# Attention and two expert layers on one core: another issue order for the five engines up to the last chunk

## The chip, the core and the metric

The kernel runs on one core of a Trainium2 chip. The metric is the device time of one execution in microseconds (us). The core's engines have a queue each and run side by side: TensorE (PE, matrix products; PEld is its loading of weights), VectorE (DVE), ScalarE (ACT), GpSimd (POOL), and SyncE (SP), which issues transfers (DMA). An engine takes its instructions in the order of its queue; one that must wait for another engine's result holds up all that stand behind it.

## The reference

Causal attention with a decay (4 batches, 8 heads, 576 positions, head size 64), whose output is the input of a feed-forward layer with a hard swish, whose output goes to a layer of eight experts, of which each token takes the one with the highest logit:

```python
scores = scale * np.matmul(q, k.transpose(0, 1, 3, 2))
decay = cum[:, :, :, None] - cum[:, :, None, :]
scores = np.where(causal, -1000000000.0, scores + decay)
attn = np.exp(scores - np.max(scores, axis=-1, keepdims=True))
attn = attn / (np.sum(attn, axis=-1, keepdims=True) + 1e-09)
x = np.matmul(attn, v)            # then 2304 tokens of 512
...
h = x @ w_in                      # 512 x 2048
g = h * np.clip(h + 3.0, 0.0, 6.0) / 6.0
x = g @ w_out                     # 2048 x 512
...
e_idx = np.argmax(x @ w_gate, axis=1)
h = np.maximum(x[mask] @ w1[e], 0.0)       # 512 x 1024
out[mask] = gate_w[mask, None] * eom[mask, e, None] * (h @ w2[e])
```

## The kernel before, in words

**Three parts.** The tokens are cut into six chunks of 384. Part one is the attention, in units of two heads and 128 positions. Part two is the feed-forward layer (`moe1_steps`), chunk by chunk; a chunk can start when all attention outputs of its tokens are there, so attention of later chunks and feed-forward products of earlier ones share the engines. Part three is the experts. To be precise enough, each factor is kept as a high part in f16 and a low part in bf16 or f16, and each product is made of three.

**An attention unit.** PE makes the scores (L457, L524, L525) in one of three PSUM tiles `sc`. DVE adds the mask and takes the row's extreme (L504, or L530 for the last positions; tile `nm`), and so frees the score tile. ACT takes the exponential (L538) and writes its high part (L555, L559, L560), POOL or DVE the low part (L556, L563). SP transposes both by DMA (L567, `pt` from `pn`). PE multiplies with the values (L590 to L592, and L602 to L605 for the last positions): these are the probability products, "pv" below, with 65 columns each. They have a single accumulator in PSUM, `ps_pv`. DVE empties it: L613 and L614 take the reciprocal of the row's sum, L615 multiplies (`evac`); for the last positions it is L627, L628 and two instructions of L631, one for each half (`evac_last`). ACT (L618) and POOL split the result `xs` into `xn`, and SP transposes that into the chunk's `xT` (L653). L399 on ACT copies rows of the keys and queries, L376 splits loaded ones.

**A feed-forward chunk.** For each of 16 steps twelve products of 384 columns (L857) fill one of three PSUM banks `mm`. ACT adds 3 and cuts at zero (L861), DVE multiplies with the bank (L864) and so gives the bank back, ACT writes the high part of `g` (L865), DVE or POOL the low part (L869). Then 4 times 48 products (L880), emptied by L889 (ACT) and L890 (DVE). The first weights come as f32 and are converted in the kernel: `conv_raw` gathers bits on DVE (L820, L822, L824), ACT writes the high part (L827), POOL or DVE the low part (L828). The gates of a chunk (`gate_steps`) are small products (L945, L977, L978) and much bookkeeping on DVE (L959 to L1000, among it the cast L994), with PSUM tiles from the same three banks `mm`.

**What sets the order.** The program is traced once, and each engine's instructions are numbered in traced order. `ORDER` (L58 to L195) holds for each of the five engines a list of runs over those numbers: "a+n" is a and the next n. `pin_order` ties each instruction to the one ahead of it in this list, so the engine issues in that order. It is called behind the tracing of the last chunk's feed-forward layer and covers all ahead of that call: 4274 of PE's products. The experts (`first = [expert1...]` and on) stand behind it, in an order of their own. `pin_order` changes no dependence between engines: an instruction that needs another engine's result waits for it wherever it stands.

Of the kernel before, what the change touches and what calls it, by code (L numbers as in the profile page):

```python
# [60 lines left out]
        "0+43 48+7 59+3 44+3 66+3 56+2 63+2 96+1 70+6 98+4 77+7 103+1 112+8 85+3 93+2 89+3 105+3 121+3 137+3 "  # L61
        "109+2 125 128+8 144+8 126+1 141+2 157 160+8 176+1 158+1 178+6 153+3 169+3 185+3 201+3 173+2 189+2 "
        "205+2 221+2 217+3 233+3 249+3 192+8 208+8 265+3 368+1 237+2 382+1 253+2 269+2 224+8 240+8 308+2 "
        "256+8 272+35 311+8 420+8 320+25 429 346+1 430+1 440+11 348+19 370+7 396+9 378+3 384+11 406+10 418+1 "
        "417 432+7 452+11 480+9 464+1 490+1 526+10 492+1 537 466+6 506+7 473+6 554+11 538+1 580+11 566+1 "
        "592+3 494+11 514+11 540+13 596+3 612+11 688+3 676+11 704+7 724+3 692+11 568+11 600+11 624+13 752 "
        "712+11 777 802 753+2 778+2 803+2 728+23 765+5 638+37 815+3 771+5 790+5 828+6 840 796 835+4 866+5 "
        "797+1 872 841 853+1 842 855 843 856 873+4 756+5 799 891+8 800+1 900+1 878+3 902 916+23 762 940+2 "
        "903+3 943+2 1024+2 763+1 781+8 1027 946+24 806+8 819+8 971+21 1049+3 993 1074+1 844+8 857+8 1076+1 "
        "994+18 1099+3 1013+1 1160+1 882+8 907+8 1015+8 1183+1 1206+3 1028+8 1053+8 1078+8 1103+8 1210+3 "  # L70
        "1037+11 1062+6 1235+1 1069+4 1087+7 1162+8 1185+8 1264+1 1095+3 1112+4 1290+7 1117+11 1322+1 1129+4 "
        "1214+8 1237+8 1134+25 1171+10 1350+1 1388+7 1266+11 1298+11 1324+13 1182 1194 1420+1 1195+10 1223+11 "
        "1460+1 1246+5 1486+7 1352+11 1396+11 1422+13 1252+6 1606 1259+4 1278+11 1310+3 1622 1314 1607+2 "
        "1623+1 1462+11 1494+11 1530+13 1625 1638+3 1315+6 1338+11 1364+11 1762+3 1544+23 1376+10 1568+13 "
        "1387 1408+11 1838+3 1863+3 1888+1 1436+23 1842+5 1890+1 1913 1474+11 1506+23 1582+6 1594 1589+1 "
        "1595+8 1591 1604+1 1610 1592+1 1611+10 1626+11 1642+33 1848 1676 1849 1677 1850 1678+7 1867 1686 "
        "1868 1687 1869 1688 1870 1689 1871 1690 1872 1691 1873 1692 1874 1693 1875 1694+22 1914 1717 1915 "
        "1892+6 1718 1899 1719 1900 1916 1720+6 1917 1727 1918 1728 1919 1729 1920 1730 1921 1731 1922 1732 "
        "1923 1733 1924 1734 1925 1735+17 1944 1753 1945 1754 1946 1755 1947 1756+5 1948+1 1766 1950 1767 "
        "1951 1768 1952 1769 1953 1969 1770 1954 1771 1955 1970 1772 1956 1971 1773 1972 1774+3 1973+2 1778 "  # L80
        "1976 1779 1977 1780 1978 1781 1979 1994 1782 1980 1783 1981 1995 1784 1996 1785 1997 1786+7 2019 "
        "1794 2020 1795 2021 1796 2022 1797+17 1998+8 2023+8 1815+22 2080+3 2105+3 1851+11 2084+7 1876 2092 "
        "1877+6 2109 1884 2110 1885 2111 1886 2112 1887 2130 2113 2131 2114 2132 2115 2133 2116 1901 2117 "
        "1902+6 2155 1909 2156 1910 2157 1911 2158 1912 1926+3 2180 1930 2181 1931 2203+1 1932+4 2134+8 "
        "2159+8 1937+1 2226+7 1939+4 1957+4 2255+1 1962+5 2182+8 2205+8 1968 2278 1982 2279 1983+10 2304+7 "
        "2007+2 2234+8 2257+8 2010+8 2032+11 2432 2448 2433 2044+3 2280+11 2312+11 2048+31 2449 2434+9 "
        "2093+11 2118+11 2143+11 2168+9 2474+7 2444 2178 2445 2179 2446 2191 2447 2192+9 2506 2202 2507 "
        "2214+11 2243+4 2450+11 2482+11 2508+10 2248 2519 2249 2520 2250 2521 2251+3 2266+11 2292+11 2324+20 "
        "2582 2345 2583 2346+5 2584 2352 2585 2353 2586 2354 2587 2355 2588 2356 2589 2357 2590 2358 2591 "
        "2359 2592 2360 2593 2361 2594 2362 2595 2363+8 2608+7 2372+11 2616 2384 2617 2385 2618 2386 2619 "  # L90
        "2387 2620 2388 2621 2389 2622 2390 2623 2391 2624 2392 2625 2393 2626 2394 2627 2395+27 2658 2423 "
        "2659 2424 2660 2425 2661 2426 2662 2427 2663 2428 2664 2429 2665 2430 2666 2431 2667+2 2462 2670 "
        "2463 2671 2464+1 2722 2466 2723 2467 2724 2468 2725 2469+4 2494+3 2738 2498 2739 2499 2740 2500 2741 "
# [1362 lines left out]
```

## Time and profile before

| | us |
|---|---|
| median of three runs | 810.03 |
| lowest and highest | 807.61, 811.63 |
| the profiled execution | 808.86 |
| its span | 807.1 |
| PE busy in the span | 726.0 |
| DVE busy | 471.5 |
| ACT busy | 450.9 |
| POOL busy | 315.6 |

The span is the time from the first to the last record of the execution's trace; 1.8 us of the profiled execution lie around it. Busy time is counted without time in which an engine waits. A group of matmuls of one kind is shown as one row with its count; its length includes the tail of the last one, which overlaps what follows. The number in square brackets behind a row is the idle time of the engine ahead of it, with the instruction that ended it. The granted clock is TensorE's: 1.00 is 2.4 GHz and 0.50 is 1.2 GHz. The first feed-forward product runs at 73.35 us.

### The profile page before, as it was taken

What the parts mean: (1) busy time and instruction counts of PE and PEld (TensorE: products, weight loads), DVE (VectorE), ACT (ScalarE), POOL (GpSimd) and SP (SyncE); (2) the same over time, 40 slices, a digit from 0 to 9 for tenths busy, and PEclk for the clock granted to TensorE, in tenths of its full rate; (3) what the DMA queues carried; (4) which work ended last, traced back from release to release, by engine and by line L of the source; (5) the groups of instructions that cost most, each with busy time, mean ns of one, the idle gap of its engine ahead of it and who ended that gap; (6) DMA issues with size and microseconds to landing.
All of it is one profiled execution on the core that took longest, in us unless ns stands there. A gap on an engine that the chain in (4) does not pass through costs nothing. (4 is left out here: it accounts for less than half of the span.)

```text
span 807.1 us, 16599 instructions
## 1 busy us (share of the span) xinstructions
PE 726.0 (90%) x6166; PEld 474.6 (59%) x6177; DVE 471.5 (58%) x1267; ACT 450.9 (56%) x909; POOL 315.6 (39%) x393
## 2 busy tenths in 40 slices
PE   4755979889899999998999889999999999999995
PEld 2533546556556655665666555666677766756862
DVE  7998987646751585229723968573142575536520
ACT  4864779857893676368824646552123465535430
POOL 9556778766663353245712420000042232220010
PEclk9986989999999999999999999999999999999999
DMA  8758799989986585469724737723068889968210
GB/s 246 221 171 200 173 198 243 211 148 165 176 162 137 121 145 115 67 124 159 131 42 91 139 79 233 245 67 105 1 168 148 237 266 295 302 200 258 82 39 28
DMA packets 263778, 127.95 MB, mean 159 GB/s; under 512 B 214658, under 2 KB 247522, under 8 KB 263684
## 3 DMA queue, kind: packets, MB, share of 16 engines
q1 hardware_dynamic: 251860, 105.20, 58.9%
q0 software_dynamic: 4960, 15.73, 6.1%
q10 hardware_dynamic: 6864, 5.80, 2.6%
q8 instruction: 54, 0.88, 0.5%
q14 instruction: 40, 0.33, 0.1%
HBM read 71.52 MB, written 10.08 MB: 101 GB/s over the span
## 5 line engine op out<-in xcount | busy, mean ns | idle before, releaser
L857 PE MATMUL mm<-xT,wi 128*128 128x384 f16 (+1 forms) x1152 | 209.3, 333 | 10.3 <-DMA xT<-xn 5.4
L880 PE MATMUL mm<-g,wo 128*128 128x384 f16 (+1 forms) x1152 | 195.7, 326 | 1.5 <-DVE hr L864 1.4
L857 PEld LDWEIGHTS <-wi 128*128 128x128 f16 (+1 forms) x1152 | 112.2, 99 | 85.2 <-issue 16.4
L880 PEld LDWEIGHTS <-wo 128*128 128x128 f16 (+1 forms) x1152 | 111.0, 98 | 73.6 <-issue 1.8
L1160 PEld LDWEIGHTS <-W 128*128 128x128 f16 (+1 forms) x1344 | 99.9, 98 | 9.1 <-issue 0.6
L556 POOL TENSOR_TENSOR pn<-ms,pn 128x384 bf16<-128x384 f32 (+1 forms) x80 | 82.6, 1037 | 56.2 <-ACT pn L555 53.2
L538 ACT ACTIVATE ms<-ms,nm 128x512 f32<-128x512 f32 (+4 forms) x144 | 79.3, 576 | 34.2 <-DVE nm L504 26.6
L1160 PE MATMUL mm<-g,W 128*128 128x256 f16 (+3 forms) x1152 | 96.6, 246 | 0.5 <-DVE wo L1164 0.5
L1179 PE MATMUL mm<-W,wo 128*128 128x512 f16 (+1 forms) x422 | 94.2, 379 | 2.4 <-ACTq L1392 1.6
L1051 DVE TENSOR_TENSOR W<-stw,W 128x1024 bf16<-128x1024 f32 x46 | 55.6, 1223 | 52.5 <-ACT W L1050 52.4
L504 DVE CUSTOM_DVE_ANT_1 ms<-sc,mask 128x128 f32<-128x128 f32 (+3 forms) x128 | 59.2, 485 | 26.5 <-PE sc L457 12.7
L1179 PEld LDWEIGHTS <-wo 128*128 128x128 f16 (+1 forms) x432 | 41.9, 98 | 52.1 <-issue 2.0
L869 DVE TENSOR_TENSOR g<-hr,g 128x384 bf16<-128x384 f32 x80 | 54.9, 688 | 29.6 <-ACT g L865 29.4
L864 DVE SCALAR_TENSOR_TENSOR hr<-hr,mm 128x384 f32<-128x384 f32 x96 | 52.7, 549 | 28.7 <-ACT hr L861 28.0
L1186 POOL DMA_INDIRECT out_dram<-wo,ids x18 | 18.0, 998 | 119.8 <-ACT wo L1185 96.5
L865 ACT ACTIVATE g<-hr 128x384 f16<-128x384 f32 x96 | 49.3, 516 | 27.3 <-DVE hr L864 26.6
L861 ACT ACTIVATE hr<-mm,bias 128x384 f32<-128x384 f32 x96 | 54.5, 568 | 16.3 <-PE mm L857 14.6
L1164 DVE SCALAR_TENSOR_TENSOR wo<-mm,wo 128x128 bf16<-128x128 f32 (+1 forms) x96 | 33.3, 356 | 46.9 <-ACT wo L1163 44.4
L590 PE MATMUL pv<-vt,pt 128*128 128x65 f16 x320 | 41.8, 197 | 20.6 <-DVE xs L615 9.8
L1050 ACT ACTIVATE W<-stw 128x1024 f16<-128x1024 f32 x46 | 47.7, 1050 | 14.5 <-DMA stw<-in_moe_w_dram 13.9
L890 DVE SCALAR_TENSOR_TENSOR x<-mm,x 128x384 bf16<-128x384 f32 x24 | 13.2, 555 | 71.9 <-ACT x L889 71.9
L457 PE MATMUL sc<-K,q 128*128 128x256 f16 (+2 forms) x192 | 46.1, 297 | 9.2 <-DVE nm L504 6.5
(191 smaller groups left out, 1179.8 us busy)
## 6 DMA issues: line engine op xcount, KB each, us to landing
stw<-in_moe_w_dram SPq DMA_DIRECT2D x46, 512.0 KB
stx<-in_moe_w_dram SPq DMA_DIRECT2D x18, 512.0 KB
wo<-in_moe_w_in_dram SPq DMA_DIRECT2D x16, 512.0 KB
raw<-in_moe_w_out_dram ACTq DMA_DIRECT2D x11, 512.0 KB
rows<-rw POOLq DMA_DIRECT2D x15, 256.0 KB, 2.9
ldk<-in_k_dram SPq DMA_DIRECT2D x14, 256.0 KB
ldq<-in_q_dram SPq DMA_DIRECT2D x14, 256.0 KB
ldv<-in_v_dram SPq DMA_DIRECT2D x13, 256.0 KB
```

Source lines behind the costliest of these rows:

```text
L504: nc.vector.tensor_tensor_reduce(out=pairs(ms[:, off:off + w]), in0=ps[:, 0:w].rearrange("p (c j) -> p c j", c=2), in1=pairs(mask[:, 640 - ...
L538: nc.scalar.activation(out=ms[:, off:off + w], in_=ms[:, off:off + w], func=AF.Exp, scale=-1.0, bias=nm[:, i:i + 1])
L556: nc.gpsimd.tensor_tensor(out=lo.bitcast(BF16), in0=ms[:, 0:N], in1=hi, op=ALU.subtract)
L857: nc.tensor.matmul(ps[:, 0:w], lhsT=l.bitcast(BF16) if a else l, rhs=r.bitcast(BF16) if b2 else r, start=i == 0, stop=i == 3 * KD - 1)
L861: nc.scalar.activation(out=hr, in_=ps[:, 0:w], func=AF.Relu, bias=bias3)
L864: nc.vector.scalar_tensor_tensor(out=hr, in0=hr, scalar=6.0, in1=ps[:, 0:w], op0=ALU.min, op1=ALU.mult)
L865: nc.scalar.activation(out=g[:, m, 0, 0:w], in_=hr, func=AF.Copy)
L869: either.tensor_tensor(out=g[:, m, 1, 0:w].bitcast(BF16), in0=hr, in1=g[:, m, 0, 0:w], op=ALU.subtract)
L880: nc.tensor.matmul(ps[:, 0:w], lhsT=l.bitcast(BF16) if a else l, rhs=r.bitcast(BF16) if b2 else r, start=i == 0, stop=i == 3 * NF - 1)
L1051: nc.vector.tensor_tensor(out=lo.bitcast(BF16), in0=sts[i], in1=hi, op=ALU.subtract)
L1160: nc.tensor.matmul(ps[:, 0:w], lhsT=l.bitcast(BF16) if a else l, rhs=r.bitcast(BF16) if b2 else r, start=i == 0, stop=i == 3 * KD - 1)
L1179: nc.tensor.matmul(ps, lhsT=l.bitcast(BF16) if a else l, rhs=r.bitcast(BF16) if b2 else r, start=i == 0, stop=i == 3 * NF2 - 1)
```

## The change

Only the strings in `ORDER` differ: the same numbers, every one once, in another succession, on all five engines. The new table is seven lines shorter, so that each line behind it has a number lower by seven (L864 of before is L857 of after). A line of it before and after:

```diff
 ORDER = {
     "PE":
-        "0+43 48+7 59+3 44+3 66+3 56+2 63+2 96+1 70+6 98+4 77+7 103+1 112+8 85+3 93+2 89+3 105+3 121+3 137+3 "
...
+        "0+31 48+7 59+3 32+15 66+3 56+2 96+1 63+2 70+6 98+4 89+3 103+1 112+8 105+3 77+11 121+3 93+2 109+2 "
...
```

PE's first difference is at its 33rd product and its last at the 4254th, near 580 us. Counted as runs of products of one kind, PE's order has 729 before and 490 after; pv products that stand alone between two feed-forward products are 190 before and 37 after. Of the other engines' instructions 829 of 1131 stand elsewhere on DVE, 525 of 766 on ACT, 208 of 359 on POOL and 165 of 326 on SP.

Three places, the first on DVE, about 108 to 112 us of the trace before. `pv_1246` is the accumulator that is emptied, `raw`, `cv`, `w32` and `wo` belong to the conversion of weights; a trailing number tells tiles of one name apart. Before, from L627 on:

```order
L627 TENSOR_SCALAR rl_1364<-pv_1246 128x2
L530 ISA ms_1433,nm_1434<-sc_1441,mask4_85,nm_1434 128x64
L530 ISA nm_1434 128x1
L824 SCALAR_TENSOR_TENSOR w32_1155<-raw_1085,cv_1156 128x512
L628 RECIPROCAL rl_1364<-rl_1364 128x2
L828 TENSOR_TENSOR wo_99<-w32_1116,wo_99 128x4x128
L820 TENSOR_SCALAR cv_1217<-raw_1123 128x512
L631 TENSOR_SCALAR xs_1365<-pv_1246,rl_1364 64x64 x2
```

After, from the same instruction on (L620 is L627 of before, L624 is L631, L813 is L820, L821 is L828):

```order
L620 TENSOR_SCALAR rl_1364<-pv_1246 128x2
L523 ISA ms_1433,nm_1434<-sc_1435,mask_84 128x2x256
L523 ISA nm_1434 128x1
L621 RECIPROCAL rl_1364<-rl_1364 128x2
L813 TENSOR_SCALAR cv_1156<-raw_1085 128x512
L624 TENSOR_SCALAR xs_1365<-pv_1246,rl_1364 64x64
L497 ISA ms_1521,nm_1522<-sc_1523,mask_84 128x2x256
L497 ISA nm_1522 128x1
L523 ISA ms_1433,nm_1434<-sc_1441,mask4_85,nm_1434 128x64
L523 ISA nm_1434 128x1
L624 TENSOR_SCALAR xs_1365<-pv_1246,rl_1364 64x64
```

L828 of `w32_1116` stood between L628 and the two L631, and now stands four rows below the last of these; one L820 is now between L628 and the first L631, and parts of an L504 and an L530 between the two L631.

The second is on ACT, about 308 to 313 us. `hr` is the feed-forward step's tile, `mm` its bank, `K2`, `kp` and `Q2`, `qp` are the next keys and queries. Before:

```order
L861 ACTIVATE hr_4255<-mm_4242,bias3_86 128x384
L399 ACTIVATE K2_94<-K1_93 64x1024
L376 ACTIVATE kp_5251<-ldk_4266 128x8x64
L538 ACTIVATE ms_4860<-ms_4860,nm_4861 128x512
L865 ACTIVATE g_97<-hr_4255 128x384
L399 ACTIVATE Q2_0_88<-q1_5116 64x1024
L376 ACTIVATE qp_5258<-ldq_4274 128x8x64
L861 ACTIVATE hr_4289<-mm_4276,bias3_86 128x384
```

After (L854 is L861 of before, L392 is L399, L369 is L376):

```order
L854 ACTIVATE hr_4255<-mm_4242,bias3_86 128x384
L392 ACTIVATE K2_94<-K1_93 64x1024
L854 ACTIVATE hr_4289<-mm_4276,bias3_86 128x384
L369 ACTIVATE kp_5251<-ldk_4266 128x8x64
L531 ACTIVATE ms_4860<-ms_4860,nm_4861 128x512
L858 ACTIVATE g_97<-hr_4255 128x384
```

L861 of `mm_4276` stood last of these, behind L399 of `Q2_0` and both L376, and now is the third, behind L399 of `K2`; the L399 of `Q2_0` stands 23 rows below it.

The third is on DVE, about 371 to 376 us, where a chunk's gates are worked out among feed-forward steps. Before:

```order
L864 SCALAR_TENSOR_TENSOR hr_5100<-hr_5100,mm_5087 128x384
L988 TENSOR_SCALAR z_5275<-z_5275 128x3
L990 TENSOR_TENSOR z_5275<-z_5275,sx_5276 128x3
L869 TENSOR_TENSOR g_97<-hr_5100,g_97 128x384
L991 RECIPROCAL z_5275<-z_5275 128x3
L994 CAST vb_5287<-z_5275 128x3
L995 CAST vals_108<-vb_5287 128x3
L864 SCALAR_TENSOR_TENSOR hr_5135<-hr_5135,mm_5122 128x384
```

After (L857 is L864 of before, L987 is L994):

```order
L857 SCALAR_TENSOR_TENSOR hr_5135<-hr_5135,mm_5122 128x384
L974 TENSOR_REDUCE z_5275<-t3_5171 128x3
L964 TENSOR_TENSOR ohsum_107<-ohsum_107,oh_106 128x8
L862 TENSOR_TENSOR g_97<-hr_5100,g_97 128x384
L975 TENSOR_REDUCE sx_5276<-t2_5170 128x3
L982 TENSOR_SCALAR sx_5276<-sx_5276 128x3
L981 TENSOR_SCALAR z_5275<-z_5275 128x3
L983 TENSOR_TENSOR z_5275<-z_5275,sx_5276 128x3
L984 RECIPROCAL z_5275<-z_5275 128x3
L987 CAST vb_5287<-z_5275 128x3
L988 CAST vals_108<-vb_5287 128x3
L857 SCALAR_TENSOR_TENSOR hr_5195<-hr_5195,mm_5182 128x384
```

L864 of `mm_5122` stood behind the cast L994 of `z_5275`, and now stands nine rows ahead of it; the next L864, of `mm_5182`, stands two rows behind the cast.

## Rows read from the trace of the kernel before

**Rows 1.** The page's head: engine, busy us (share of the span) x instructions.
```profile
PE 726.0 (90%) x6166; PEld 474.6 (59%) x6177; DVE 471.5 (58%) x1267; ACT 450.9 (56%) x909; POOL 315.6 (39%) x393
```

**Rows 2.** By stage: start:end, length, busy PE, PEld, DVE, ACT, POOL, granted clock.
```profile
0.00:73.35 73.35, 38.33 (x333) 27.29 (x334) 66.22 (x163) 44.61 (x93) 46.15 (x82) 0.86 0.75 213
73.35:480.00 406.65, 372.18 (x3262) 236.77 (x3262) 250.93 (x771) 268.88 (x567) 218.72 (x262) 0.98 0.75 142
480.00:800.00 320.00, 315.54 (x2573) 210.49 (x2581) 154.36 (x335) 137.42 (x250) 49.76 (x49) 1.00 0.59 170
```

**Rows 3.** The same view of seven stretches of the second stage.
```profile
100.00:135.00 35.00, 28.76 (x240) 18.39 (x239) 29.14 (x84) 28.92 (x62) 28.73 (x33) 0.90 1.12 219
140.00:150.00 10.00, 7.55 (x57) 4.63 (x55) 8.51 (x26) 9.23 (x20) 7.82 (x9) 1.00 1.24 254
160.00:180.00 20.00, 15.84 (x172) 10.15 (x171) 9.02 (x35) 12.59 (x30) 13.45 (x21) 0.97 0.74 153
195.00:230.00 35.00, 29.50 (x297) 19.65 (x294) 24.53 (x88) 30.13 (x66) 23.39 (x29) 0.95 0.97 174
285.00:315.00 30.00, 26.98 (x250) 16.68 (x247) 21.34 (x67) 24.21 (x50) 16.36 (x20) 1.00 0.90 157
360.00:405.00 45.00, 39.64 (x376) 26.42 (x372) 35.14 (x114) 38.57 (x90) 28.42 (x36) 0.96 0.80 141
450.00:475.00 25.00, 18.66 (x205) 12.53 (x203) 20.68 (x65) 13.38 (x31) 11.52 (x17) 1.00 0.59 110
```

**Rows 4.** PE's waits, 75 to 480 us: us in total, times, longest.
```profile
PE pv L590 <- DVE xs L631: 7.4, 4, 3.7
...
PE mm L857 <- DVE hr L864: 4.8, 3, 1.8
```

**Rows 5.** Busy time in four stretches at the low clock: the first, the sum.
```profile
110.60:117.40 6.80, 5.25 (x49) 3.98 (x50) 6.75 (x16) 3.76 (x9) 5.69 (x7) 0.50 1.18 175
...
sum 17.00, PE 15.18 PEld 9.74 DVE 12.58 ACT 11.03 POOL 9.32; mean PE 3.79 PEld 2.43 DVE 3.15 ACT 2.76 POOL 2.33
```

**Rows 6.** DVE in order of time, 105 to 112 us: start, length, instruction.
```profile
105.38 0.69 DVE L820 TENSOR_SCALAR cv<-raw 128x512 int32<-128x512 int32 x1 [1.06 <-DMA raw<-in_moe_w_out_dram]
...
107.45 0.15 DVE L627 TENSOR_SCALAR rl<-pv 128x2 f32<-128x2 f32 x1
...
109.25 1.67 DVE L828 TENSOR_TENSOR wo<-w,wo 128x512 bf16<-128x512 f32 x1 [0.77 <-ACT wo L827]
...
111.44 0.57 DVE L631 TENSOR_SCALAR xs<-pv,rl 64x64 f32<-64x64 f32 x2
```

**Rows 7.** PE in order of time, at 112 us.
```profile
112.15 0.21 PE L590 MATMUL pv<-vt,pt 128*128 128x65 f16 x1 [3.67 <-DVE xs L631]
```

**Rows 8.** ACT in order of time, 311 to 313 us.
```profile
311.06 1.05 ACT L399 ACTIVATE Q<-q 64x1024 f16<-64x1024 f16 x1
...
312.66 0.56 ACT L861 ACTIVATE hr<-mm,bias 128x384 f32<-128x384 f32 x1
```

**Rows 9.** DVE in order of time, 299 to 378 us.
```profile
299.97 0.56 DVE L864 SCALAR_TENSOR_TENSOR hr<-hr,mm 128x384 f32<-128x384 f32 x1
...
373.16 2.40 DVE L994 CAST vb<-z 128x3 bf16<-128x3 f32 x1
...
377.40 0.55 DVE L864 SCALAR_TENSOR_TENSOR hr<-hr,mm 128x384 f32<-128x384 f32 x1
```

**Rows 10.** PE in order of time, 296 to 370 us.
```profile
296.16 0.33 PE L857 MATMUL mm<-xT,wi 128*128 128x384 f16 x1
...
299.92 0.19 PE L590 MATMUL pv<-vt,pt 128*128 128x65 f16 x1
...
300.47 1.95 PE L857 MATMUL mm<-xT,wi 128*128 128x384 f16 x11
...
369.41 0.32 PE L857 MATMUL mm<-xT,wi 128*128 128x384 f16 x1
```

**Rows 11.** One line's instructions: duration ns shortest/median/longest, first and last start.
```profile
L828 DVE TENSOR_TENSOR wo<-w,wo x11: 681/819/2333, 79.6 to 150.8; 128x512 bf16<-128x512 f32 x11
```

249 rows, old and new, of the table ORDER are left out of this document.

## The prediction

> **What bounds the kernel now.** I read first the head of the page [rows 1]: TensorE (PE) is busy for 726.0 of 807.1 us, so what the order can change is at most the 81 us in which it is not. Then the busy time by stage [rows 2] says where these lie. To 73.35 us, where the first feed-forward product runs, PE works 38.33 us, but VectorE (DVE) works 66.22: this stage is DVE's. From 73.35 to 480 us PE works 372.18 of 406.65 us, and 34.5 us are waits. From 480 to 800 it is idle for 4.5 us in 320, and the last 7.1 us are the store of the result. The table covers the first two stages and the feed-forward products of the third, so the 34.5 us are the change's stock. I cut the second stage into the seven stretches in which its waits lie [rows 3]: length less PE's busy time gives 6.2, 2.5, 4.2, 5.5, 3.0, 5.4 and 6.3 us, 33.1 of the 34.5. The waits view [rows 4] says for whom: in all 34 waits of about 1.0 us each; the largest group is probability products (pv) that wait for DVE to empty their one accumulator (L631, 7.4 us), and another is feed-forward products that wait for DVE's L864, which gives a PSUM bank back (4.8 us). They are waits for queues that had something else in front. Last, the clock: behind four of the waits the granted clock is 0.50, the lower of its two levels, for 17.0 us in all, in which PE is busy 15.18 us [rows 5]; half of it, 7.6 us, is the price of the level.
>
> **The change, part by part.** It removes and adds no instruction: the same work stands in another order on five queues. What PE does costs the same: eighteen pv products from 299.92 to 300.47 take 0.03 us each, and eleven feed-forward products take 1.95 us of which the last one's 0.33 is mostly its tail, 0.16 us each [rows 10]. So each stretch counts by its waits.
>
> 100 to 135 us (6.2). A pv product waits 3.67 us, to 112.15 [rows 7]. It is held by the second half of L631. Before it DVE has a conversion L828 of 1.67 us, and from L627 at 107.45 to that second half at 111.7 it needs 4.3 us; earlier the same queue stood 1.06 us for a transfer, at an L820 [rows 6]. In the new DVE order the L820 with that transfer stands behind the sum of this pv (L615), and L828 and the next L820 stand behind both halves of L631. From L627 to the second half stand the first part of an L530, an L628, one L820, the first half, an L504 and the rest of the L530, by the lengths of such rows some 3.0 us: 1.3 less. And L627 itself no longer has two conversion steps of 0.69 us and the 1.06 us wait ahead of it. I take 3.2 off (1.3 to 3.67). The other waits here, 1.8 us, are of a score tile that PE now issues some 9 us of its work later: 1.5 off. 4.7 in all.
>
> 140 to 150 (2.5). Scores and pv move 8.6 and 6.5 us of PE work back, and both waits are shorter than that: 2.0 off. 160 to 180 (4.2): a pv stood straight behind the one whose accumulator it needs and now has 2.9 us of work between, and the first product of the next chunk has 8.7 us behind its last pv instead of 4.2: 3.2 off. 195 to 230 (5.5): the largest is a wait for a transposing transfer that SyncE (SP) now issues six places earlier and PE reads 2.5 us of work later; the others, small ones, are spread: 2.0 off.
>
> 285 to 315 (3.0). ScalarE (ACT) takes the L861 of the product that holds a bank at 312.66, behind an L399 of 1.05 us [rows 8]; the new order puts this L861 ahead of that L399 and of both L376: its wait of 1.79 us goes, 1.8 off. 360 to 405 (5.4): DVE's L864 stands behind a cast L994 that took 2.40 us at 373.16 [rows 9]; it now stands nine places ahead of the cast, and ACT's L861 in front of it has moved ahead by seven: of this wait and three others 3.6 off. 450 to 475 (6.3): L631 moves six places up on DVE, and the scores behind the transfer at the end 2.3 us up on PE: 3.0 off.
>
> The sum is 4.7 + 2.0 + 3.2 + 2.0 + 1.8 + 3.6 + 3.0 = 20.3 us. Of the clock's 7.6 us I take half, since a wait that is cut short need not vanish: 3.8. Together 24.1. From below I hold it at 12 (each wait half-solved, its remainder met by the next reader of the same engine), from above at all 33.1.
>
> What the new order costs lies in the same queues. By counting PE's work (0.16 us a product, 0.03 a pv) between a bank's or accumulator's last product and its next use, the old order has no bank reused within 3 us of work, the new one six, with 2.0 to 2.9 us; accumulators reused within 3 us go from three to seven, and gate tiles from none to three within 2.5. What the path through ACT and DVE takes there is seen in before: from a product's end at 296.49 to the end of L864 at 300.53 is 4.0 us, and from 369.73 to 377.95 it is 8.2 [rows 9, 10]. But these long paths were long where nobody waited, and in the new order DVE has its L864, L631 and L628 a mean of 1.2 to 1.7 us earlier in the order of work, since conversions and gate bookkeeping stand later. Ten of the thirteen added short places at the mean wait of 1.0 us are 10, and before's waits show that places over 3 us wait too: 3 more. I take 13 (0 to 19, the latter if each of the sixteen met the path that before shows for its own instruction).
>
> The start is taken at nothing: DVE has the same work ahead of the first chunk's last sum, and PE's first product stands behind that; since DVE is busy for 66.22 of 73.35 us [rows 2], only a new stall there could be seen, 2 us either way. The work behind 480 us and the tail are not moved; a shift of their loads has 4.5 us of idle time to show in, and is nothing.
>
> Where VectorE meets GpSimd (POOL), the same L828 took 681 ns at the least and 2333 at most [rows 11], and the cast of three numbers 2.40 us [rows 9]. The Trainium skill, "SBUF — State Buffer", section "SBUF: two separate sides", says that a VectorE operation which uses the port pair that it shares with GpSimd blocks for the whole of the other's instruction. The rows agree that such an operation stretches, though one POOL instruction does not show 2.40 us. By that rule a new neighbour can stretch any of them: a cast stretched again to 2.40 us stands two places ahead of the next L864 in the new order, and if that made PE wait for all of it, the gains would be 21.7 in place of 24.1 and the time 801.4.
>
> **The rivals.** *The waits change places.* Each engine has much to do where PE waits: in 360 to 405 ACT works 38.57 of 45 us and DVE 35.14 [rows 3]. Then half of the 24.1 comes, 12, and the 13 are paid: 809.9, and against the median 811, no change. Against it: the solved waits had a named instruction in front, which does move behind.
>
> *Banks come back too late: slower.* It is the six places of reuse at 2.0 to 2.9 us (mean 2.35) of PE work. If the path there takes what it took in before's crowded places, 4.0 to 8.2 [rows 9, 10], mean 6.1, each costs 3.75, together 22.5; with 7 us for the ten accumulators and gates, and three more stretches at the low clock, each like those of [rows 5] at about 1.7, 5, it is 34.5 against 24.1: 808.9 + 10.4 = 819.3, or 820 by the median. It decides from a path of about 4.4 us: there the banks cost 12 and the sum is nil. For it: the path was 4.0 at one of the very products in question, and ACT and DVE are not idle. Against it: L864 and L861 come earlier on their engines.
>
> *Longer runs of one kind.* The new order has 490 runs of equal PE work in place of 729, and single pv between two feed-forward products fall from 190 to 37. By [rows 10] that alone is worth under 0.5 us, since a pv costs 0.03 us in a run. The Trainium skill, "Perfetto Trace Analysis", section "Matmul Optimizations", says that products should run back to back in batches, because the engine's power follows its use. The trace has the clock at 0.98 in this stage [rows 2] with these single pv in it; all that this could add is the other half of the clock's 7.6 us, to 795. I count this in the range of the forecast, with no chance of its own.
>
> **How the numbers follow.** The profiled execution took 808.86 us, 1.8 more than its span, and 1.2 less than the median of 810.03. 808.9 - 24.1 + 13 = 797.8; with 1.2 for the median it is 799.0. Chances: 0.62 for this; 0.20 that the waits change places (811); 0.18 for the banks (820). The range: with nothing of the 13 paid it is 784.8 + 1.2 = 786; below lies less than one in ten. Upward it takes in the second case and the banks' case to near half of its price, 815; one in ten lies above. Within 0.5%, 4 us, is about what a measurement of this kernel can tell from no change: faster by more 0.62, within it 0.20, slower by more 0.18.
>
> **What would show it.** In the changed kernel's profile the waits of PE between the first feed-forward product and the last chunk should sum to about 27 us (34.5 - 20.3 + 13), those for L631 to under 4 in place of 7.4, and no pv should wait over 2 us around 110. If the forecast is wrong through the banks, the group of L857 behind L864 grows from 4.8 to over 15; if the waits only change places, the sum stays at 32 or more with other names. The granted clock of that stage should be 0.98 to 1.0. The first feed-forward product should run at 71 to 75 us; if it runs later than that, the start was not nothing, and DVE's idle time before it names the cause. The busy time of PE from 480 to the end should be the same to 1 us.

## The result and the profile after

The changed kernel takes 797.36 us (median of six runs, 795.17 to 799.48) against 810.74 for the kernel before, run beside it (six runs, 803.89 to 812.58): a ratio of 0.985, 95% interval 0.981 to 0.989. The forecast was 799.0. The profiled execution took 799.48 us, its span 797.8, so that the two traces stand 9.3 us apart where the medians stand 13.4; the traces below account for the 9.3. The profiled execution of the kernel after is the slowest of its six. Every line behind the table has a number lower by seven. The head of the page, beside [rows 1]:

```profile
span 797.8 us, 16631 instructions
...
PE 724.9 (91%) x6177; PEld 476.1 (60%) x6177; DVE 473.8 (59%) x1267; ACT 450.6 (56%) x909; POOL 317.7 (40%) x393
```

The work is the same on each engine to about 2 us; the time went out of PE's gaps. To see where, I cut both traces at the same points of PE's order: at the first feed-forward product, and at two places where both orders have issued the same set of products. Stages (columns as in [rows 2]), first the kernel before:

```profile
73.35:188.00 114.65, 100.39 (x815) 61.69 (x814) 84.29 (x223) 85.63 (x176) 85.13 (x95) 0.94 0.96 191
188.00:475.65 287.65, 267.44 (x2424) 172.45 (x2422) 163.68 (x541) 180.46 (x385) 132.74 (x166) 0.99 0.67 123
```

And the kernel after:

```profile
0.00:70.99 70.99, 38.71 (x334) 29.23 (x335) 64.72 (x161) 43.41 (x92) 45.47 (x81) 0.82 0.80 220
70.99:187.60 116.61, 101.36 (x820) 62.69 (x820) 84.92 (x223) 85.76 (x177) 84.98 (x93) 0.92 0.93 181
187.60:465.20 277.60, 264.28 (x2419) 171.29 (x2419) 167.09 (x540) 182.12 (x385) 134.74 (x168) 0.99 0.74 131
```

The first feed-forward product comes 2.4 us earlier; the stretch from there to 188 us is 2.0 longer (116.61 for 114.65); the next, to 475.65 of before, is 10.05 shorter (277.60 for 287.65); behind it 1.1 are lost. Of the 10.05, the idle time (length less PE's busy time) gives 20.2 - 13.3 = 6.9, and PE's busy time 3.2. Whose waits are left, from the first feed-forward product to 480 us (columns as in [rows 4]):

```profile
PE mm L850 <- DVE hr L857: 8.2, 8, 2.5
PE pv L595 <- DMA pt<-pn: 6.7, 2, 5.5
PE pv L583 <- DMA pt<-pn: 4.3, 3, 2.9
PE pv L583 <- DVE xs L624: 3.5, 3, 1.7
PE mm L850 <- DMA xT<-xn: 3.3, 1, 3.3
PE sc L450 <- DVE Q L390: 2.2, 1, 2.2
...
PE mm L873 <- DVE hr L857: 2.1, 2, 1.3
```

Waits for the accumulator that end on L624 (L631 of before) fell from 7.4 to 3.5 us, all waits that end on DVE's L857 (L864 of before), mostly for a bank, grew from 8.5 to 10.3, and the largest single wait is a new one: 5.5 us for a transposing transfer. All groups sum to 33.0, or 29.7 without the 3.3 of the first feed-forward product. At the low clock there is as much time as in [rows 5]; the longest of four stretches, and the sum:

```profile
120.60:127.40 6.80, 3.54 (x23) 2.75 (x24) 2.35 (x8) 3.50 (x9) 2.75 (x5) 0.50 1.16 192
...
sum 17.00, PE 13.74 PEld 8.17 DVE 10.12 ACT 12.43 POOL 9.82; mean PE 3.44 PEld 2.04 DVE 2.53 ACT 3.11 POOL 2.46
```

Again 17.00 us. PE was busy for 13.74 of them, 15.18 before: half of the difference, 0.7 us, is what the clock gave. One of the four stretches lies behind 188 us (281.0) where before had two.

The 5.5 us in the trace, PE first and then ACT's DMA issues some 10 us ahead of it (a row's length is the second number):

```profile
123.86 0.29 PE L595 MATMUL pv<-vt,pt 128*128 128x130 f16 x1 [5.53 <-DMA pt<-pn]
```

```profile
113.88 0.37 ACTq L799 DMA_DIRECT2D raw<-in_moe_w_out_dram  x1
...
114.62 0.44 ACTq L799 DMA_DIRECT2D raw<-in_moe_w_out_dram  x1
```

Two weight loads of 512 KB go out 0.74 us apart, and the transposes that PE waits for were issued at 114.09, 0.2 us behind the first load, and at 115.89, behind both. The next large one, SP's queue and then PE:

```profile
157.93 6.16 SPq L342 DMA_DIRECT2D ldv<-in_v_dram  x2
164.19 3.94 SPq L560 DMA_TRANSPOSE pt<-pn  x3
```

```profile
167.30 0.20 PE L583 MATMUL pv<-vt,pt 128*128 128x65 f16 x1 [2.90 <-DMA pt<-pn]
```

SP spends 6.16 us at two loads of values, and the three transposes stand behind them.

### The profile page after: what moved, and what is told of

Read it like the earlier page. It is cut to its first block, busy times and chain, and to the rows that moved or that the text cites. A ratio compares the mean times of both kernels' runs of the same rounds, so it can differ in the third digit from the quotient of the medians.

```text
span 797.8 us, 16631 instructions
## 1 busy us (share of the span) xinstructions
PE 724.9 (91%) x6177; PEld 476.1 (60%) x6177; DVE 473.8 (59%) x1267; ACT 450.6 (56%) x909; POOL 317.7 (40%) x393
## 5 line engine op out<-in xcount | busy, mean ns | idle before, releaser
L497 DVE CUSTOM_DVE_ANT_1 ms<-sc,mask 128x128 f32<-128x128 f32 (+3 forms) x128 | 60.8, 485 | 31.5 <-PE sc L450 18.1
L862 DVE TENSOR_TENSOR g<-hr,g 128x384 bf16<-128x384 f32 x80 | 58.8, 738 | 22.0 <-ACT g L858 21.8
L854 ACT ACTIVATE hr<-mm,bias 128x384 f32<-128x384 f32 x96 | 54.8, 571 | 21.9 <-PE mm L850 15.1
L857 DVE SCALAR_TENSOR_TENSOR hr<-hr,mm 128x384 f32<-128x384 f32 x96 | 52.7, 549 | 24.2 <-ACT hr L854 23.8
L1156 ACT ACTIVATE wo<-mm 128x128 f16<-128x128 f32 (+1 forms) x96 | 31.4, 330 | 39.6 <-PE mm L1153 33.6
```

The costliest lines, as they stand in the source:

```text
L497: nc.vector.tensor_tensor_reduce(out=pairs(ms[:, off:off + w]), in0=ps[:, 0:w].rearrange("p (c j) -> p c j", c=2), in1=pairs(mask[:, 640 - ...
L854: nc.scalar.activation(out=hr, in_=ps[:, 0:w], func=AF.Relu, bias=bias3)
L857: nc.vector.scalar_tensor_tensor(out=hr, in0=hr, scalar=6.0, in1=ps[:, 0:w], op0=ALU.min, op1=ALU.mult)
L862: either.tensor_tensor(out=g[:, m, 1, 0:w].bitcast(BF16), in0=hr, in1=g[:, m, 0, 0:w], op=ALU.subtract)
```

## The experiments

Below, a kernel's **lead** is worked out from two traces: the start of a product at a point of PE's order where both have issued the same set of products, less the same in before. Negative is ahead. In us:

| at (before's time) | after | new order behind 187 only | new order to 187 only | new order to 231 only | four repairs | eight repairs |
|---|---|---|---|---|---|---|
| 73.35 | -2.4 | -0.9 | -4.8 | -3.7 | -2.6 | -3.7 |
| 125.6 | +0.4 | -2.9 | -5.2 | -4.9 | -4.0 | -5.7 |
| 188.2 | -0.6 | -1.5 | -5.1 | -5.6 | -4.9 | -10.4 |
| 226.5 | -5.9 | -6.6 | -1.5 | -9.3 | -10.7 | -14.7 |
| 280.1 | -6.1 | -6.8 | -3.2 | -0.9 | -11.2 | -15.1 |
| 376.4 | -6.9 | -7.7 | -0.4 | +1.3 | -12.5 | -16.9 |
| 475.7 | -10.5 | -10.6 | -1.8 | -0.8 | -15.1 | -23.5 |
| 579.9 | -9.3 | -9.9 | -1.5 | -0.6 | -13.7 | -22.7 |

Each column is a single execution, and two executions can differ by some 5 us with the same order. Five kernels have after's order up to 187 us; at 188.2 their traces stand at -0.6 (after), -0.3 (after, once more), -5.1 (new order to 187 only), -5.6 (new order to 231 only) and -5.1 (two places undone, below). The first feed-forward product gives 1.3 to 3.6 us of that. Another 3.1 to 3.6 arise between 80 and 90 us, at one DVE copy: it takes 3.52 us in both traces of after, and 0.27 in the other three; a part of both comes back later. DVE of after, then of two places undone:

```profile
80.86 3.52 DVE L390 COPY K2t<-K1t 64x512 f16<-64x512 f16 x1
```

```profile
80.68 0.27 DVE L391 COPY K2t<-K1t 64x512 f16<-64x512 f16 x1
```

In after PE waits 2.2 us behind it (the group of L390 above), and then has 0.53 of the clock from 87.5 to 90; two places undone has 1.00 at the same work, from 83.5 to 85. So a lead says something only where it is larger than this, or where the times of several runs bear it out. From the first feed-forward product to 188 us the five traces gain -1.8, -1.0, 0.3, 1.9 and 1.0 us.

**Three places alone.** The kernel before, with the three moves of the front's order listings made by hand, each in its place and nothing else:

```diff
 DVE, about 109 us
+L631 TENSOR_SCALAR xs<-pv,rl 64x64 x2
 L828 TENSOR_TENSOR wo<-w_1116,wo 128x4x128
 L820 TENSOR_SCALAR cv<-raw 128x512
-L631 TENSOR_SCALAR xs<-pv,rl 64x64 x2
 ACT, about 309 us
+L861 ACTIVATE hr<-mm,bias_86 128x384
 L376 ACTIVATE kp<-ldk 128x8x64
...
-L861 ACTIVATE hr<-mm,bias_86 128x384
 DVE, about 373 us
+L864 SCALAR_TENSOR_TENSOR hr<-hr,mm 128x384
 L994 CAST vb<-z 128x3
 L995 CAST vals<-vb 128x3
-L864 SCALAR_TENSOR_TENSOR hr<-hr,mm 128x384
```

> The kernel before, with three local moves of the new table and nothing else: on DVE both L631 at 111 us stand ahead of L828 and the L820 behind it; on ACT the L861 at 312.66 us stands behind the first L399, ahead of both L376 and the second L399; on DVE the L864 at 375.68 stands ahead of the cast L994. Theory of the prediction (a wait goes when the instruction in front of its releaser goes): the three waits of 3.67, 1.79 and 1.85 us shrink by 2.9, 1.8 and 1.8, together 6.5, and the low clock behind the first and last gives back up to 2: 802 to 804 beside a before of 810. Rival (waits change places, above all from the wait at 112 to the transposing transfers read at 124): the three go, but PE's sum of waits between 75 and 480 us falls by under 3 us: 808 to 810.

Measured: 812.63 us (ten runs) against 811.97 (19), ratio 1.000 (0.997 to 1.003). The rival holds: PE's waits from 75 us on, less that of the first product, sum to 37.2 us for 34.3 in before. But the three places differ. In time order, PE, DVE, PE and DVE of this kernel:

```profile
108.14 0.19 PE L590 MATMUL pv<-vt,pt 128*128 128x65 f16 x1 [0.75 <-DVE xs L631]
```

```profile
142.84 0.69 DVE L820 TENSOR_SCALAR cv<-raw 128x512 int32<-128x512 int32 x1 [3.54 <-DMA raw<-in_moe_w_out_dram]
```

```profile
145.52 0.37 PE L457 MATMUL sc<-K,q 128*128 128x256 f16 x1 [3.35 <-DVE nm L504]
```

```profile
370.86 3.34 DVE L967 TENSOR_TENSOR oh<-t,cm 128x24 f16<-128x24 f32 x1
```

The wait of [rows 7] shrinks from 3.67 to 0.75, and PE runs 4.0 us ahead at 108. Then DVE, which has also become earlier, stands 3.54 us at an L820 for a weight load (1.41 at that L820 in before), and the scores behind it wait 3.35: the lead is +1.2 at 145. At the second place 1.9 us come off and stay. At the third the wait behind the cast is gone, but the one at the feed-forward step ahead of it grew from 1.64 to 3.40, since now an L967 is stretched to 3.34.

**The place at 112, kept.** To the kernel of the experiment above, three L820 (with L822 or L824) moved behind the scores and sums queued after them:

```diff
-L820 TENSOR_SCALAR cv_1319<-raw_1232 128x512
 L504 ISA ms_1906,nm_1907<-sc_1908,mask_84 128x2x64
...
 L864 SCALAR_TENSOR_TENSOR hr_1820<-hr_1820,mm_1807 128x384
+L820 TENSOR_SCALAR cv_1319<-raw_1232 128x512
```

> The three local moves on the old table, with more of DVE's order moved between 126 and 147 us: three L820 that stood waiting for a weight load (0.96, 1.03 and 3.54 us in the three moves' trace) and their L822 and L824 stand behind the score tiles and sums that were queued behind them. In that trace the 4.0 us that were won at 112 were lost by 145.52, where a score waited 3.35 us for an L504 behind such an L820. Theory (DVE stands for the weight load, and PE for what is queued behind it): the wait at 145.52 falls under 1 us and 3 of the 4 us stay: 808 to 810 beside 812.6 for the three moves and 810 to 812 for before. Rival (the feed-forward products that need those weights wait instead): 811 to 814.

Measured: 812.14 (ten runs), ratio 1.000 (0.997 to 1.003). The wait at 145.5 is gone and the lead there is -1.4 instead of +1.2, but 16 us later it is +1.1. PE's waits from 105 to 182 us (this kernel's lines are one lower than before's):

```profile
PE sc L456 <- DVE nm L503: 3.2, 4, 1.4
PE pv L589 <- DVE xs L614: 2.7, 2, 1.4
PE sc L456 <- ACT Q L398: 1.9, 1, 1.9
PE mm L856 <- DMA xT<-xn: 1.4, 1, 1.4
```

The whole view has fifteen waits, 13.9 us, none above 1.9; before has fourteen in that stretch, 12.8 us, the largest 3.67. The large wait went and others took its place; only this one was tried.

**Longer runs alone.** PE's order of before, in which single pv products between two feed-forward products are drawn together where nothing forbids it (132 such places become 2, and 818 runs of one kind become 581, about as many as after has by the same count); the other four engines keep their order.

> The kernel before, with PE's order alone changed: where single pv products alternate with feed-forward products, the same products stand as one run of feed-forward and one of pv, each such run ending where it ended before. By one count single pv between feed-forward products fall from 132 to 2 and runs of one kind from 818 to 581, which is the changed kernel's number. Theory of the prediction (a pv costs 0.03 us alone or in a run, the order is worth only the waits it moves): within 1.5 us of before, 809 to 811. Rival (longer runs of one kind are what made the changed kernel faster, through the clock or the queue of PE): 798 to 802.

Measured: 810.20 (ten runs) against 811.97, ratio 0.999 (0.996 to 1.002). Longer runs of one kind are worth nothing that can be measured here (the interval leaves up to some 3 us). The page cited for it, the Trainium skill's "Perfetto Trace Analysis", section "Matmul Optimizations", asks for batches; no run here shows a gain from them.

**After, once more.**

> The changed kernel unaltered, for its trace a second time: how far the single waits repeat. If the waits belong to the order, the 5.53 us at 123.86, the 2.90 at 167.30, the 2.51 at 280.24 and the first feed-forward product at 70.99 come again within 1 us. If the stretching of DVE instructions beside POOL or the landing of transfers is chance, they move by more: 795 to 800 either way.

One execution, 800.93 us. It is slower than each of the six runs above; the first feed-forward product came at 72.11, 1.1 later. The two large waits for transfers repeat: 5.53 became 4.90, 2.90 became 3.10. A later one does not: 0.81 became 2.37. What causes the bank wait at 280 us (2.51 in one trace, 2.41 in the other) does not repeat either: the DVE instruction that is stretched in front of L857 is the L993 shown further down in one, and in the other an operation on three columns:

```profile
124.41 0.29 PE L595 MATMUL pv<-vt,pt 128*128 128x130 f16 x1 [4.90 <-DMA pt<-pn]
```

```profile
277.17 3.81 DVE L981 TENSOR_SCALAR z<-z 128x3 f32<-128x3 f32 x1
```

**Three tables spliced.** All five orders change from one table to the other at a point that both reach with the same instructions issued: before's up to 187 us and then after's; after's up to 187 and then before's; after's up to 231 and then before's.

> Both tables spliced: all five engines in the old order for what began before 187 us in the trace of before, the rest in the new order. The two traces side by side have the changed kernel at the same point of PE's order 0.6 us earlier at 187 us and 9.3 us earlier at 580. Theory (a gain belongs to the stretch in which the order lets PE wait less, and what lies ahead of 187 us gives back what it gains): 801 to 803 beside a before of 810 to 812, that is 8 to 9 us off. Rival (the gain needs the new order as a whole, the early part preparing the late): under 4 us off, 806 to 810.

> The complement: the new order for what began before 186.2 us in the trace of after, the old order behind that. Theory: 0 to 2 us off, 809 to 811. Rival (the start, where the first feed-forward product ran 2.4 us earlier, carries on to the end): 3 us or more off, 805 to 808.

> The new order for what began before 223.7 us in the trace of after (231.3 in before), the old order behind that. At this point the changed kernel is 7.6 us ahead in the traces. Theory: 6 to 8 us off, 803 to 805, and with the run before this one it puts 6 to 7 us on the stretch 187 to 231 alone. Rival (time that PE wins is taken back by the other engines within the next stretch, as it was behind the three local moves): 2 us or less off, 808 to 811.

Measured, against 810.23 (19 runs): 797.91 (four runs, ratio 0.982, 0.977 to 0.988); 812.85 (ten, 1.003, 1.000 to 1.005); 812.11 (ten, 1.003, 1.000 to 1.006). The new order behind 187 alone gives the whole gain, as far as the runs can tell (797.91 beside 797.36). To 187 alone it gives none, by its interval 0 to 4 us of loss, although its trace is 5.1 ahead at 188: 6.6 are lost in the 16 us behind the seam. What that lead is worth where the new order goes on stays open, since two places undone keeps its 5.1 and both traces of after have the long copy. The third is the telling one: at 226 us it is 9.3 ahead, and at 280 it is 0.9 ahead. Its waits from 215 to 282 us (lines one lower than before's):

```profile
PE sc L456 <- DVE nm L503: 3.2, 2, 2.9
PE pv L590 <- POOL vt L479: 2.1, 1, 2.1
PE mm L879 <- DVE hr L863: 1.2, 1, 1.2
PE pv L589 <- DVE xs L630: 1.2, 1, 1.2
```

At that seam PE stands at the same product in both traces, but the others don't: in the new order DVE has begun 401 of its instructions of the table where the old has 414, ACT 348 for 356, POOL 203 for 209, SP 145 for 153. At 187 the counts are 313 and 313, 278 and 278, 173 and 175, 118 and 121. A reading that fits is that the 9.3 us were borrowed: work that PE did not yet wait for had been put off, and in the old order behind the seam it was wanted. It is argued and not shown: no run moves that work alone, and at 187 a lead was lost too, with equal counts. The rows of this execution name two instructions that were late, POOL's and DVE's:

```profile
224.76 0.56 POOL L954 DMA_DIRECT2D rows<-rw  x1 [5.61 <-DMA rw<-x]
```

```profile
226.42 5.18 DVE L868 TENSOR_TENSOR g<-hr,g 128x384 bf16<-128x384 f32 x1
```

POOL stood 5.61 us for a transfer, DVE waited 3.30 for POOL behind it, and then an L868 that takes 0.55 us elsewhere took 5.18 beside a row of POOL; the wait for `nm` (2.9 of the 3.2) stands behind that.

**Repairs, four and then eight.** Each moves what stood in the queue that a wait of after ends on; PE's order stays. The first four:

```diff
 ACT, about 110 us: a weight load away from the next one
+L799 DMA raw<-in_moe_w_out_dram 128x4x256
 L854 ACTIVATE hr<-mm,bias_86 128x384
 L548 ACTIVATE pn<-ms 128x512
...
-L799 DMA raw<-in_moe_w_out_dram 128x4x256
 SP, about 160 us
+L560 DMA_TRANSPOSE pt<-pn 128x6x128 x3
 L342 DMA ldv<-in_v_dram 64x8x64
-L560 DMA_TRANSPOSE pt<-pn 128x6x128 x3
 DVE, about 277 us: L993 behind the next two L857
-L993 TENSOR_TENSOR M<-vals,oh 128x168
...
+L993 TENSOR_TENSOR M<-vals,oh 128x168
 DVE, about 360 us
+L857 SCALAR_TENSOR_TENSOR hr<-hr,mm 128x384
 L958 TENSOR_TENSOR t_5169<-t_5169,rev 128x24
 L621 RECIPROCAL rl<-rl 128x2
-L857 SCALAR_TENSOR_TENSOR hr<-hr,mm 128x384
```

> The changed kernel, with four moves at its own new waits: on ACT one weight load L799 stands six places earlier (it went out at 113.88 us, 0.7 us ahead of the next such load, and the transposes behind both were read late, wait 5.53 at 123.86); on SP two transposes and a third stand ahead of an L342 load that held them from 158.3 to 163.5 us (waits 2.90, 0.61, 0.81 from 167.30); on DVE the bookkeeping L993, 3.12 us beside four POOL instructions at 276.60, stands behind two L857 (wait 2.51); and an L857 stands ahead of an L958 of 3.05 us at 359.65 (wait 0.65). Theory (each new wait has one named instruction in front): these waits fall by 3, 3.5, 2.5 and 0.6, together 9 to 10 us: 787 to 789 beside 797. Rival (the engines and the DMA are full there, so that a wait that is taken away comes up behind the next instruction): PE's waits fall by under 4 us in all: 794 to 797.

Measured: 794.17 (four runs), ratio 0.979 (0.973 to 0.984); the interval overlaps that of after, and the traces stand 4.4 us apart at 579.9. What each did, ACT, PE and DVE of this kernel:

```profile
109.69 0.37 ACTq L799 DMA_DIRECT2D raw<-in_moe_w_out_dram  x1
...
113.92 0.39 ACTq L799 DMA_DIRECT2D raw<-in_moe_w_out_dram  x1
```

```profile
119.98 0.23 PE L595 MATMUL pv<-vt,pt 128*128 128x130 f16 x1 [1.90 <-DMA pt<-pn]
```

```profile
272.01 3.92 DVE L981 TENSOR_SCALAR z<-z 128x3 f32<-128x3 f32 x1
```

One load 4.2 us earlier, and the wait for the transposes is 1.90 in place of 5.53; lead 4.4 better at 125.6 and kept. On SP the 2.90 is gone, but a later wait for `pt` is 3.19, against 0.81 in after; that one changes by itself (2.37 in after once more). On DVE the bank wait moved one product on: with L993 out of the way, the L981 behind it took 3.92 us. The wait of 0.65 that L857 ahead of L958 was to take away is gone too, but it is also absent from the second trace of after, so nothing is shown of this move.

The second four: one more transpose ahead of an `xT` and an `ldv` on SP; L857 ahead of L981 and L982 at 270 us; L857 ahead of four gate instructions (L983 to L988) at 373; an accumulator's emptying (L607 to L624) ahead of L987 and L989 at 440.

```diff
-L857 SCALAR_TENSOR_TENSOR hr<-hr,mm 128x384
+L857 SCALAR_TENSOR_TENSOR hr<-hr,mm 128x384 x2
 L981 TENSOR_SCALAR z<-z 128x3
 L982 TENSOR_SCALAR sx<-sx 128x3
-L857 SCALAR_TENSOR_TENSOR hr<-hr,mm 128x384
```

> The four repairs with four more, at waits that they left: on SP a transpose stands ahead of an xT transpose and an L342 load (wait 3.19 us at 168.38 of the four repairs' trace); on DVE an L857 stands ahead of two small L981 and L982, the first of which took 3.92 us beside POOL (wait 2.27 at 276.51); an L857 stands ahead of four small gate instructions (1.72 at 366.19); and the L624 pair ahead of two more (1.69 at 450.13). Theory (each wait has one instruction in front): 2.5 + 2.2 + 1.0 + 1.5 = 7.2 off against the four repairs, 786 to 788. Rival (about half of what is moved comes back at the next reader, as with the four repairs, whose 9 to 10 us came out as 3): 790 to 792. If DVE's stretching beside POOL is a wait for POOL's whole run of instructions, another small DVE instruction takes 3 to 4 us at 272 to 276 in place of L981.

Measured: 787.39 (four runs, 784.98 to 789.42), ratio 0.971 (0.967 to 0.976): below after's interval, and faster than both kernels. Its stages at the same two points of PE's order:

```profile
69.60:177.70 108.10, 99.62 (x818) 61.90 (x817) 82.68 (x222) 84.61 (x175) 83.55 (x93) 0.94 1.00 193
177.70:452.20 274.50, 264.55 (x2419) 171.50 (x2419) 164.11 (x540) 182.40 (x387) 135.83 (x169) 0.99 0.74 133
```

8.5 of the gain on after's trace lie ahead of 187 us, where after had gained nothing, and 3.1 behind it. Not all of the 8.5 is the repairs': the copy of 3.52 us in after takes 0.27 here, and no repair touches it. Beside the three traces with the short copy this stretch is 5 to 6 us shorter. The first group of the waits for banks halves (7.8 in after over the same times):

```profile
PE mm L850 <- DVE hr L857: 4.1, 7, 0.8
```

**POOL's row broken.** In the kernel with eight repairs, two stores L948 on POOL, which wait for a transfer and so gather POOL's work behind them, moved five instructions later.

```diff
-L948 DMA rows<-rw 128x1024
 L612 TENSOR_TENSOR xn<-xs,xn 128x128
...
 L549 TENSOR_TENSOR pn<-ms,pn 128x384
+L948 DMA rows<-rw 128x1024
```

> The eight repairs, with POOL's order changed at two places: a store of token rows (L948) that waits for its own transfer stood at the head of six and of five POOL instructions, and now stands behind five of them. In the eight repairs' trace POOL began such a row of instructions at 268.38 us, and DVE's L981 of three numbers, begun at 268.87, ended at 272.21 with the last but one of them; an L862 took 2.90 us at 216.41. Theory (a DVE instruction that meets POOL waits until POOL's unbroken row of instructions ends, and the row is unbroken because the store in front held it up): both shrink to 1.3 us or less, PE's wait of 1.99 us at 272.40 goes, 784 to 786 beside 787.4. Rival (the stretching has nothing to do with the length of POOL's row): a small DVE instruction takes 3 us there again, 787 to 788.

Measured: 786.66 (four runs), ratio 0.969 (0.964 to 0.974), not to be told from the kernel it changes. The stretched L981 is short, but not for the reason that was tried: POOL still works without a break around it.

```profile
268.92 0.91 POOL L549 TENSOR_TENSOR pn<-ms,pn 128x384 bf16<-128x384 f32 x1
269.80 0.81 POOL L612 TENSOR_TENSOR xn<-xs,xn 128x128 bf16<-128x128 f32 x2
```

```profile
269.97 0.27 DVE L981 TENSOR_SCALAR z<-z 128x3 f32<-128x3 f32 x1
```

Summed over 70 to 480 us, what DVE's instructions take above the shortest of their form (those over 0.3 us above it) is 29.0 in before, 30.3 in after, 27.7 with the eight repairs and 22.6 here, in one trace each. The stretching is less, and PE's end does not show it.

**Two places undone.** After, with the second and third place of the listings put back: ACT's L854 of `mm_4276` three rows later, DVE's L857 of `mm_5122` behind the two casts.

```diff
 ACT
-L854 ACTIVATE hr_4289<-mm_4276,bias3_86 128x384
 L369 ACTIVATE kp_5251<-ldk_4266 128x8x64
...
+L854 ACTIVATE hr_4289<-mm_4276,bias3_86 128x384
 DVE
-L857 SCALAR_TENSOR_TENSOR hr_5135<-hr_5135,mm_5122 128x384
...
 L988 CAST vals_108<-vb_5287 128x3
+L857 SCALAR_TENSOR_TENSOR hr_5135<-hr_5135,mm_5122 128x384
```

> The changed kernel with two of its places put back: on ACT the L854 at 306.88 us stands three instructions later (behind L369, L531 and L858), and on DVE the L857 at 367.32 stands behind the cast L987 and its follower L988, as in the old order. Theory (behind 187 us a place counts in full to the end): the first brings back a wait of 1.0 to 1.8, the second one of 1.5 to 2.3, 800 to 801 beside 797.4. Rival (other waits absorb them): within 1 us of 797.4.

Measured: 798.38 (four runs), ratio 0.985 (0.980 to 0.991): the time cannot tell it from after. The trace can (lines one higher than after's):

```profile
303.20 0.32 PE L851 MATMUL mm<-xT,wi 128*128 128x384 f16 x1 [1.17 <-DVE hr L858]
...
363.42 0.17 PE L971 MATMUL mm<-oh,tri 128*128 128x8 f16 x1 [1.54 <-DVE hr L858]
```

Both waits came back, although the trace is of the fastest of the four runs, 792.65. The first stays as 1.3 us to 370; the second is met by later waits that shrink (1.72 to 0.88, and 0.80 to none).

## Why the prediction was right, and where it was not

**The sum held; its parts did not.** 799.0 was forecast, 797.36 measured. But of the seven stretches the first three, up to 180 us, were to give 9.9 us, and they gave nothing of that size: the five traces with after's order there gain -1.8 to 1.9 us from the first feed-forward product to 188, the new order to 187 alone measures 1.003, and the new order behind it has the whole gain.

**The step that failed there** is the one used against the rival "waits change places": "the solved waits had a named instruction in front, which does move behind". It did move (waits for L624 are 3.5 us, under the 4 that was named, and no pv waits over 2 us near 110), and other queues took its place. Ahead of 187 idle time of PE that is not the first product's went from 14.1 to 15.1 us by the waits view of after, 2.2 of them at the copy that is long in two of the five traces. Two others of the new waits come from moves that the prediction did not read: two weight loads that ACT issues together (5.53), and SP's transposes behind a load of values (2.90). For these stretches the working read DVE's queue and the distances on PE, and neither SP's queue nor the DMA issues on ACT's. So this rival, given 0.20, is what happened in the first third of the stage.

**Behind 187** the steps were 2.0 + 1.8 + 3.6 + 3.0 = 10.4, and the trace's stretch is 10.05 shorter; by the splice it is 12.3 us of the medians (810.23 - 797.91). The removal was more complete than half, and new waits were paid for it: of the 20.2 us of idle time 13.3 are left, and eight waits for L857 have 9.1 of them. They are not of the predicted kind, which was a bank or accumulator used again within 3 us of PE's work. Of the ten waits for L857 up to 480 us, 10.3 us, two stand at such a place (0.83 at 299.45 with 2.04 us of work between, 1.72 at 371.78 with 2.62); the path through ACT and DVE took 2.8 and 4.3 us there, under the 4.4 from which the second rival was to decide. At the other eight 4.4 to 7.6 us of work lie between, and the path took 4.8 to 8.3. The waits for the accumulator have 3.3 to 14.3 us of work between. So the second rival did not come true at its six places; what is left are long paths at places that are not short. The two single steps that were tried stand in the right direction: undone in after, they bring back 1.17 and 1.54, where 1.8 and part of 3.6 had been taken; made alone in before, the first gives 1.9 and the second is met by the next stretched instruction.

**The clock** was mis-sized: 3.8 were taken, and 17.00 us lie at the low level as before, worth 0.7. New long waits (5.53 with the stretch from 120.60) put it there in place of the old ones. PE's busy time behind 188 fell by 3.2 all the same; the one low stretch fewer is worth 1.7 of them, and for the other 1.5 no row names a cause.

**The new waits** were taken at 13 and the sum of waits at about 27; 29.7 are left, so by this measure the forecast was 2.7 too low, and under the 32 that would have been the first rival's. The size was near; the kind was not. The 13 were counted from banks and accumulators, and the waits for these fell, from 18.5 us in before to 14.0. Waits for transposing transfers rose from 6.3 to 11.0, and 2.2 came at the copy at 80 us; for these the working had no term. **The start** was taken at nothing, 2 either way; the first feed-forward product came at 70.99, 2.4 us earlier, and in the other traces with the same order there 1.3 to 4.8 earlier. Of the 4.8 (new order to 187 only) nothing that the runs can tell is left at the end. **Work behind 480** is as said: PE is busy for 315.75 us from 470 to 800, 315.54 from 480 to 800 in [rows 2]. **Longer runs of one kind** are worth nothing that the runs can tell, as the prediction had it.

That the sum came out is in part luck: 9.9 us of gains ahead of 187 that were not there and 3.1 too much for the clock stand against 13 charged as new waits, which the two stretches' balances of +2.0 and -10.05 hold already. That these 13 came near what is left is luck too, since ten of them were counted from short places, where PE's waits for banks came to 2.55 us and those for the accumulator to nothing.

## What to carry to other kernels

When an order is changed, read a gain at the end of the stage and not at the wait that went: a lead of one engine can be lost again, by the reading above where the other queues had done less. Take more than one trace: one lead of PE can differ by 5 us from another of the same order. For each wait that is to go, list every queue that ends on the waiting instruction, DMA issues on two queues included, since the next latest one sets the time. A further gain of some 10 us lay in repairing the new waits (787.4 us), each by moving what stood in front in the queue that ended last.

## What the runs showed of the hardware

A DVE instruction can stand for as long as POOL works without a break, over several of its instructions. In after, DVE and then POOL:

```profile
276.60 3.12 DVE L993 TENSOR_TENSOR M<-vals,oh 128x168 bf16<-128x168 f32 x1
```

```profile
276.60 0.92 POOL L549 TENSOR_TENSOR pn<-ms,pn 128x384 bf16<-128x384 f32 x1
...
278.73 0.80 POOL L612 TENSOR_TENSOR xn<-xs,xn 128x128 bf16<-128x128 f32 x2
```

L993 starts with POOL's row and ends at 279.72, where the row ends at 279.5 (L993 takes 0.33 us in the other trace of after). PE paid 2.51 us for it:

```profile
280.24 0.32 PE L850 MATMUL mm<-xT,wi 128*128 128x384 f16 x1 [2.51 <-DVE hr L857]
```

In the kernel with eight repairs an operation on 128x3 numbers does the same, to 272.21, with POOL's row ending at 272.18:

```profile
268.87 3.34 DVE L981 TENSOR_SCALAR z<-z 128x3 f32<-128x3 f32 x1
```

```profile
268.38 0.93 POOL L549 TENSOR_TENSOR pn<-ms,pn 128x384 bf16<-128x384 f32 x1
...
271.28 0.90 POOL L549 TENSOR_TENSOR pn<-ms,pn 128x384 bf16<-128x384 f32 x1
```

The Trainium skill, "SBUF — State Buffer", section "SBUF: two separate sides", speaks of one POOL instruction's length; the two rows of POOL here have five and six instructions. It is not so each time: the L981 of 0.27 us above lies within such a row, and which instruction is stretched changes between two executions of one kernel. The copy at 80 us is another case: 3.52 us in two executions, with a row of POOL that ends 0.1 us ahead of it, and 0.27 in others with the same order. What decides it stays open.

Transposing transfers that are issued just behind two loads of 512 KB are late by several microseconds. The wait for them is 5.53, 4.90, 5.66, 4.77 and 4.61 us in the five traces with after's order there, and 1.90, 3.10 and 2.77 in the three with the first of the loads 4.2 us ahead of the second. In after the transposing transfers' packets land at 85 to 152 per half microsecond from 119 to 123 us, while packets of the loads run, and at 458 and 495 in the two halves behind 123.5.
